# Row tiles in plain order with indexed gathers and chunk-layout copies, instead of rotated and mirrored access patterns

## The chip, the cores and the metric

One core of a Trainium2 chip runs the whole program. The metric is the device time of one execution in microseconds (us). Before the change its median over 3 runs is 2033.77 us (2030.04 to 2036.78).

## The reference

A transformer block with a spectral mixer is computed forward, and then its gradients by all inputs but one:

```
x = A_x
mod = (silu(c) @ w_mod).reshape(c.shape[0], 6, 1, -1)        # sa, ca, ga, sb, cb, gb
h = layernorm(x) * (1 + ca) + sa
x = x + ga * irfft2(rfft2(h) * (w_r + 1j * w_i))             # spectral filter, 2048 x 1024
h = layernorm(x) * (1 + cb) + sb
x = x + gb * (gelu(layernorm(h) @ w1 + b1) @ w2 + b2)        # 1024 -> 3584 -> 1024
out, vjp = jax.vjp(block, A_x, A_w_r, A_w_i, w1, b1, w2, b2, c, w_mod)
return out, *vjp(grad_out)
```

`A_x` and `grad_out` have 2048 rows of 1024 bfloat16 values; `w_r` and `w_i` have 2048 rows of 513.

## The kernel before

The work is written with a tile framework: the code names tiles and operations, and the framework gives every engine its own in-order queue, sets all waits, and lays out each queue by priority and by the time at which it expects an operation to be ready. An engine's order therefore need not be that of the code, but once laid out it is fixed: what waits holds everything behind it on its queue. SyncE's queue (SP) issues loads and DMA transposes, GpSimd's (POOL) issues most stores.

The two-dimensional Fourier transforms are matrix multiplications with cosine and sine matrices that the kernel generates at its start (`trig`, `gen_mats`) and keeps in DRAM (`d_SF`, `d_E`). To make them small, rows are folded: a row tile holds rows n, 2047-n, 1023-n and 1024+n together. Tile i (of 4) has four quarters q of 128 rows each: q = 0 and 3 in natural order (rows 128 i and 1024 + 128 i on), q = 1 and 2 in mirrored order (from row 2047 - 128 i and 1023 - 128 i downwards). `fold_tok`, `fold_d`, `unfold_tok` and `unfold_d` (VectorE) add and subtract quarters and halves of rows.

The stages, in the order of the code:

1. Modulation rows (`mod_block`, L190: 1 MiB blocks `wblkA` and `wblkB` of `w_mod`), loads of `grad_out` (`go`, four tiles) and of `A_x` (`x4`, four tiles in two buffers, `load_x`, L484), generation of the matrices, `d_gBo` = gradient times `gb` (L507) and its DMA transposes `gBoT` (L511), layer norm and folding of x (L522 to L533).
2. Spectral forward (`spectral_core`, L349): `s_fwd`; eight `pair` steps (L354), each of which loads 128 rows of `w_r` and `w_i` twice (`w_plus`, L138, and mirrored `w_minus_parts`, L142) into `ws`, multiplies, and stores `d_P`; `s_inv`; then per row tile the last product into `po`, evacuated by ScalarE (L466), and `consume_fwd` (L543), which loads x again (L547) and stores `d_A`, `d_x1`, `d_n3`.
3. The product of the gradient with the second weight (L573, `wt` by DMA transposes of `B_w2`, result to `d_ph`). It only needs `gBoT` and fills TensorE beside stage 2.
4. The MLP forward and the gradient through the gelu (`z_block`, L599; `bo_pass`, L635, eight of them: `w2` loads L643, half row tiles of `grad_out` L651, `out_0` stored from GpSimd L659).
5. The gradient through the first weight and the layer norms (L706 to L750), per block of 4 x 128 rows: loads of `n3u`, `n2u` and the gradient tile `go4` (L731); stores `d_gx1`.
6. Spectral backward: the same `spectral_core`. Its `pair` steps also load `d_P` into `pf` (L406) and store the gradients of `w_r` and `w_i` (`out_2`, `out_3`) from GpSimd (L414, L416). `consume_bwd` (L771) loads x (L780) and `d_gx1` (L791) and stores `out_1` (L793).
7. Weight gradients: `gw2` (L817, fills TensorE beside stage 6), the gradient of the modulation (L849 to L861), `gw1` (L887).

Everything that reads or writes a row tile goes through `tok_aps` (L116). It puts the rows of a tile on partitions rotated by 64, so that a mirrored quarter is written as two blocks of 64 rows with a row step of -1:

```
out.append((bass.AP(tensor=th, offset=off + r0 * D, ap=[[D, 64], [1024 * D, 2], [1, w]]),
            t4[64 * half:64 * half + 64, 0:4:3, :]))
...
out.append((bass.AP(tensor=th, offset=off + r0 * D, ap=[[64 * D, 2], [-D, 64], [1, w]]), t4[:, q, :]))
```

So a row tile is four DMAs: two of 64 partitions for the natural quarters, and one of 128 rows for each mirrored quarter, whose pattern begins with a dimension of 2. `w_plus` has the same form (128 rows, beginning with a dimension of 2), `w_minus_parts` is two or three DMAs of up to 64 rows. The Fourier matrices are generated for this rotated order (`kev`, `kod`, `rown`, L260 to L272).

Of the kernel before, what the change touches and what calls it, by code (L numbers as in the profile page):

```python
# [16 lines left out]
P = 128  # L17
# [17 lines left out]
def kernel(  # L35
# [62 lines left out]
    d_A = dram.tile([S, D], BF16, name="d_A")  # L98
    d_n3 = dram.tile([S, D], BF16, name="d_n3")
    d_gBo = dram.tile([S, D], BF16, name="d_gBo")  # L100
    d_gx1 = dram.tile([S, D], BF16, name="d_gx1")
# [13 lines left out]

    def tok_aps(dram_, t4, i, c0, c1):  # L116
        s3 = dram_[0] if len(dram_.shape) == 3 else dram_
        th, off = s3.tensor, s3.offset + c0
        lo, w = 128 * i, c1 - c0
        out = []  # L120
        for half in range(2):
            r0 = lo + 64 * (1 - half)
            out.append((bass.AP(tensor=th, offset=off + r0 * D, ap=[[D, 64], [1024 * D, 2], [1, w]]),
                        t4[64 * half:64 * half + 64, 0:4:3, :]))
        for q, top in ((1, 2047), (2, 1023)):
            r0 = top - lo - 64
            out.append((bass.AP(tensor=th, offset=off + r0 * D, ap=[[64 * D, 2], [-D, 64], [1, w]]), t4[:, q, :]))
        return out

    def load_tok(eng, t4, src, i, c0=0, c1=D):  # L130
        for dr, sb in tok_aps(src, t4, i, c0, c1):
            eng.dma_start(out=sb, in_=dr)

    def store_tok(eng, dst, t4, i, c0=0, c1=D):
        for dr, sb in tok_aps(dst, t4, i, c0, c1):
            eng.dma_start(out=dr, in_=sb)  # L136

    def w_plus(w, par, m):  # L138
        r0 = 256 * m + 128 - par
        return bass.AP(tensor=w.tensor, offset=w.offset + r0 * DF, ap=[[128 * DF, 2], [-2 * DF, 64], [1, DF]])  # L140

    def w_minus_parts(w, par, m):  # L142
        out = []
        for half in range(2):
            r0 = 2048 - 256 * m - 128 * (1 + half) + par
            lo = 0
            if half == 1 and par == 0 and m == 3:
                lo = 1
                out.append((64, 65, w[0:1, :]))
            out.append((64 * half + lo, 64 * half + 64,  # L150
                        bass.AP(tensor=w.tensor, offset=w.offset + (r0 + 2 * lo) * DF, ap=[[2 * DF, 64 - lo], [1, DF]])))
        return out

# [105 lines left out]

    kevi = iota([[128, 4], [64, 2], [-1, 64]], 64, 0, 512)  # L260
    kev = to_f(kevi, 512)
    kevc = to_f(kevi, 512)
    nc.gpsimd.memset(kevc[:, 448:449], 0.0)
    kod = gview(512, FP32)
    pts(kod, kev, 2.0, -1.0, ALU.mult, ALU.add)
    pidx = iota([[0, 1]], 64, 1, 1)
    pi2 = gview(1, I32)
    nc.vector.tensor_scalar(out=pi2, in0=pidx, scalar1=127, scalar2=None, op0=ALU.bitwise_and)
    pif = to_f(pi2, 1)
    rown = gview(4, FP32)  # L270
    for i in range(4):
        pts(rown[:, i:i + 1], pif, 2.0, float(256 * i + 1), ALU.mult, ALU.add)  # L272
    rowd = to_f(iota([[256, 2]], 1, 2, 2), 2)
# [75 lines left out]
    def spectral_core(fwd, fb, sms, em, css, pt, evac_u, evac_c, evac_v, consume, o4tag, pfs=None):  # L349
# [4 lines left out]
        def pair(n, par, m):  # L354
            ws = ws2[:, n % 2]
            for x, w in ((0, A_w_r), (1, A_w_i)):
                nc.sync.dma_start(out=ws[:, x, 0, 0:DF], in_=w_plus(w, par, m))
                for lo, hi, src in w_minus_parts(w, par, m):
                    nc.sync.dma_start(out=ws[lo:hi, x, 1, 0:DF], in_=src)
            cs = css[n % 2]  # L360
# [16 lines left out]
            tt(Pt[:, 0:4:3, :], cv[:, 0], cv[:, 1], ALU.subtract)  # L377
            sp_m = par == 0 and m == 3
            if sp_m:
                nc.vector.tensor_copy(out=Pt[64:65, 2:4, :], in_=cv[64:65, 0])  # L380
                nc.vector.tensor_scalar(out=Pt[64:65, 0, :], in0=cv[64:65, 1, 0], scalar1=-1.0, scalar2=None, op0=ALU.mult)
                nc.vector.tensor_copy(out=Pt[64:65, 1, :], in_=cv[64:65, 1, 1])
            Pv = Pt.rearrange("p (s r) w -> p s r w", r=2)[:, :, :, 0:DF]
# [17 lines left out]
            if sp_m:  # L401
                nc.vector.tensor_copy(out=R[64:65, rc, :, 0:DF], in_=qa[64:65, 1, :, 0:DF])
                nc.vector.tensor_copy(out=R[64:65, rs, :, 0:DF], in_=qa[64:65, 0, :, 0:DF])
            if not fwd:
                pf = pfs[n % 2]
                nc.sync.dma_start(out=pf.rearrange("p s r w -> p (s r w)"), in_=d_P[n])  # L406
                m1 = qb2[:, 0]
                m2 = qb2[:, 1]
                tt(m1[:, :, :, 0:DF], Pv, pf[:, :, :, 0:DF], ALU.mult)
                tt(m2[:, :, :, 0:DF], Pv, pf[:, :, ::-1, 0:DF], ALU.mult)  # L410
                tt(pf[:, 0, :, 0:DF], m1[:, :, 0, 0:DF], m1[:, :, 1, 0:DF], ALU.add)
                tt(pf[:, 1, :, 0:DF], m2[:, :, 0, 0:DF], m2[:, :, 1, 0:DF], ALU.subtract)
                for x, w in ((0, out_2), (1, out_3)):
                    nc.gpsimd.dma_start(out=w_plus(w, par, m), in_=pf[:, x, 0, 0:DF])  # L414
                    for lo, hi, dst in w_minus_parts(w, par, m):
                        nc.gpsimd.dma_start(out=dst, in_=pf[lo:hi, x, 1, 0:DF])  # L416

# [62 lines left out]


    x4s = {}
# [152 lines left out]
    def bo_pass(b, h):  # L635
# [22 lines left out]
        tt(bo, bo, x1t, ALU.add)  # L658
        store_tok(nc.gpsimd, out_0, bo, b, h * KH, (h + 1) * KH)  # L659

# [45 lines left out]
    for b in range(NB):  # L706
# [23 lines left out]
        go4 = got[:, 0:4, :]  # L730
        load_tok(nc.sync, go4, grad_out, b)  # L731
        for i in range(4):
# [38 lines left out]
    def consume_bwd(i, o4, tmp, n1):  # L771
# [7 lines left out]
        unfold_tok(o4, tmp)  # L779
        load_tok(nc.sync, n1, A_x, i)  # L780
        norm_act(n1, n1, 0, i)
# [10 lines left out]
        tt(o4, o4, n1, ALU.add)  # L792
        store_tok(nc.gpsimd, out_1, o4, i)  # L793
        if i == 3:
# [130 lines left out]
```

## Time and profile before

| | |
|---|---|
| median of 3 runs | 2033.77 us (2030.04 to 2036.78) |
| the profiled execution, its time | 2022.19 us |
| its span, first to last instruction | 2020.1 us |
| mean granted TensorE clock | 0.88 |
| busy: TensorE / VectorE / ScalarE / GpSimd | 1532.0 / 989.2 / 824.7 / 277.5 us |
| DMA queue of SyncE (hardware) | 362930 packets, 230.27 MB, 46.5% of 16 engines |
| DMA queue of GpSimd (software) | 43040 packets, 108.20 MB, 15.7% |
| row tile loads of x and gradient (L132) | 112 issues |

The views used below: the page (busy time of each engine; the span in 40 slices, each digit the busy share in tenths), windows (busy time of each engine in a stretch), the timeline (start, duration, engine, line, operation, and in brackets how long the engine had been idle and what ended that), the waits (engine and line, what it waited for: total, times, longest), and the groups of instructions (busy time, mean ns). SPq is SyncE's queue: its rows are issues of DMAs, whose duration is that of the issue and not of the transfer. The profile has no landing time for SyncE's DMAs; they are seen in who waits for them.

### The profile page before, as it was taken

How to read it: one execution, taken by the hardware profiler on the slowest of the kernel's cores; microseconds unless marked ns; L12 is line 12 of the kernel's file. 1: busy time of each engine (PE TensorE's matmuls, PEld its weight loads, DVE VectorE, ACT ScalarE, POOL GpSimd, SP SyncE). 2: the span in 40 equal slices, each digit the busy share in tenths (PEclk: the TensorE clock that was granted, in tenths of full speed). 3: DMA queues.
4: the chain of work that ended last, by engine and by line, in shares of the span. 5: the costliest groups of instructions: out<-in, count | busy, mean ns of one | idle time of the engine just before them, and what ended most of it. 6: DMA issues, size and time to landing. Idle time of an engine off the chain costs nothing. (4 is left out here: it accounts for less than half of the span.)

```text
span 2020.1 us, 18395 instructions
## 1 busy us (share of the span) xinstructions
PE 1532.0 (76%) x6722; PEld 686.1 (34%) x6722; DVE 989.2 (49%) x1381; ACT 824.7 (41%) x1095; POOL 277.5 (14%) x423
## 2 busy tenths in 40 slices
PE   2113898767998999999679898376568879925998
PEld 0001354333443344444234343133223334412443
DVE  1143274555138876666403678638555542265100
ACT  2335454676466655555203333243333322263000
POOL 3210010111211111111100000003200111032111
PEclk7556899888999999999889999687788989967999
DMA  6396468568546675656996432545534788598541
GB/s 175 124 214 157 89 159 220 141 209 195 144 120 198 205 227 186 216 188 197 219 247 150 156 122 92 162 102 127 178 97 99 148 226 203 165 331 254 124 122 37
DMA packets 406060, 339.64 MB, mean 168 GB/s; under 512 B 257477, under 2 KB 343493, under 8 KB 405842
## 3 DMA queue, kind: packets, MB, share of 16 engines
q1 hardware_dynamic: 362930, 230.27, 46.5%
q0 software_dynamic: 43040, 108.20, 15.7%
q8 instruction: 52, 0.85, 0.2%
q14 instruction: 38, 0.31, 0.0%
HBM read 168.34 MB, written 112.26 MB: 139 GB/s over the span
## 5 line engine op out<-in xcount | busy, mean ns | idle before, releaser
L887 PE MATMUL gw1acc<-gzs,n3n 128*128 128x512 bf16 x896 | 199.3, 386 | 59.9 <-ACT gwo L891 43.8
L573 PE MATMUL pp<-gBoT,wt 128*128 128x512 bf16 x896 | 209.9, 392 | 31.4 <-ACT phr L575 15.9
L720 PE MATMUL pg<-w1T,gzr 128*128 128x512 bf16 x896 | 201.9, 386 | 4.9 <-DMA gzr<-d_gz 4.8
L887 PEld LDWEIGHTS <-n3n 128*128 128x128 bf16 x896 | 89.0, 99 | 169.8 <-issue 67.3
L158 DVE TENSOR_TENSOR ct<-ct 128x2048 bf16<-128x2048 bf16 (+1 forms) x76 | 103.4, 1388 | 85.5 <-ACT ct L466 62.6
L573 PEld LDWEIGHTS <-wt 128*128 128x128 bf16 x896 | 90.9, 102 | 142.6 <-issue 29.9
L612 PEld LDWEIGHTS <-w 128*128 128x128 bf16 x896 | 87.5, 98 | 122.1 <-issue 20.4
L720 PEld LDWEIGHTS <-gzr 128*128 128x128 bf16 x896 | 89.1, 100 | 115.7 <-issue 8.6
L575 ACT CAST phr<-pp 128x512 bf16<-128x512 f32 x112 | 63.0, 588 | 131.6 <-PE pp L573 71.5
L158 DVE TENSOR_TENSOR gt<-gt,gt 128x2048 bf16<-128x2048 bf16 x84 | 101.9, 1222 | 19.0 <-ACT gt L619 18.1
L647 PEld LDWEIGHTS <-hhA 128*128 128x128 bf16 x704 | 69.5, 99 | 119.4 <-issue 39.1
L612 PE MATMUL pz<-n3Tb,w 128*128 128x512 bf16 x448 | 101.8, 383 | 6.0 <-ACT gt L614 6.0
L817 PE MATMUL gw2acc<-gB,hhsA 128*128 128x512 bf16 x448 | 102.9, 390 | 3.7 <-DMA hhsA<-d_hh 3.7
L817 PE MATMUL gw2acc<-gB,otl 128*128 128x512 bf16 x448 | 102.0, 386 | 3.4 <-ACT gwo L819 3.4
L612 PE MATMUL pz<-n3Ta,w 128*128 128x512 bf16 x448 | 99.9, 379 | 5.5 <-ACT gt L614 5.5
L614 ACT ACTIVATE gt<-pz,b_col 128x512 bf16<-128x512 f32 x112 | 74.5, 682 | 51.3 <-PE pz L612 51.3
L464 PE MATMUL po<-gm,V 128*128 128x256 bf16 x256 | 48.0, 339 | 61.9 <-ACT ct L466 61.6
L429 PE MATMUL pv<-smi,R 128*128 128x512 bf16 x256 | 63.6, 399 | 37.3 <-DVE R L158 36.6
L893 DVE CAST gwo<-gw1acc 128x512 bf16<-128x512 f32 x28 | 19.3, 690 | 148.1 <-PE gw1acc L887 148.1
L576 POOL DMA_DIRECT2D d_ph<-phr x56 | 40.0, 715 | 317.2 <-ACT phr L575 300.8
L891 ACT CAST gwo<-gw1acc 128x512 bf16<-128x512 f32 x28 | 16.3, 584 | 157.8 <-PE gw1acc L887 140.5
L819 ACT CAST gwo<-gw2acc 128x512 bf16<-128x512 f32 x56 | 32.5, 581 | 110.8 <-PE gw2acc L817 109.1
(228 smaller groups left out, 2429.3 us busy)
## 6 DMA issues: line engine op xcount, KB each, us to landing
d_ph<-phr POOLq DMA_DIRECT2D x56, 256.0 KB, 4.6
d_gz<-gt POOLq DMA_DIRECT2D x28, 512.0 KB, 5.1
gzr<-d_gz SPq DMA_DIRECT2D x28, 512.0 KB
wrw<-in_w_mod_dram SPq DMA_DIRECT2D x48, 256.0 KB
out_dram<-gww POOLq DMA_DIRECT2D x48, 256.0 KB, 4.7
d_hh<-hhA POOLq DMA_DIRECT2D x22, 512.0 KB, 4.8
w2sA<-in_B_w_dram SPq DMA_DIRECT2D x19, 512.0 KB
w2sB<-in_B_w_dram SPq DMA_DIRECT2D x19, 512.0 KB
```

What stands on the lines that cost most here:

```text
L158: nc.vector.tensor_tensor(out=out, in0=a, in1=b, op=op)
L429: nc.tensor.matmul(pv[:], lhsT=R[:, cl * 4 + m, :, :].rearrange("p x w -> p (x w)")[:, base:base + 255:2], rhs=smi[:, cl // 2, m, :], star ...
L464: nc.tensor.matmul(po[:, d2 * 256:(d2 + 1) * 256], lhsT=Vs[cl][:, 2 * dc + h, i * P:(i + 1) * P], rhs=gm[:, gi, :], start=(h == 0), stop=( ...
L573: nc.tensor.matmul(pp[:], lhsT=w2t[:, cch, k * P:(k + 1) * P], rhs=gBoT[b][:, cch, :], start=(cch == 0), stop=(cch == NDC - 1))
L575: nc.scalar.copy(out=ph2[:, k, :], in_=pp[:])
L576: nc.gpsimd.dma_start(out=d_ph_v[:, 2 * fg:2 * fg + 2, b * BW:(b + 1) * BW], in_=ph2)
L612: nc.tensor.matmul(pz[:], lhsT=w1s[cch][:, fc * P:(fc + 1) * P], rhs=n3T[:, cch, :], start=(cch == 0), stop=(cch == NDC - 1))
L614: nc.scalar.activation(out=zb[:, k, :], in_=pz[:], func=ACT.Identity, bias=b1_col[:, fc:fc + 1], scale=1.0)
L647: nc.tensor.matmul(pbs[i][:], lhsT=hh[:, k, i * P:(i + 1) * P], rhs=wp[:, k, :], start=False, stop=(g == 6 and k == 3))
L720: nc.tensor.matmul(pgs[i][:], lhsT=gzt[g][:, k, i * P:(i + 1) * P], rhs=w1Ts[g][:, k, h * KH:(h + 1) * KH], start=(g == 0 and k == 0), sto ...
L817: nc.tensor.matmul(acc[:], lhsT=hhs[:, t, k * P:(k + 1) * P], rhs=gBs[t // 4][:, t % 4, h * KH:(h + 1) * KH], start=(t == 0), stop=(t == N ...
L887: nc.tensor.matmul(acc[:], lhsT=n3ns[t // 4][:, t % 4, cch * P:(cch + 1) * P], rhs=gzs[:, t, :], start=(t == 0), stop=(t == NT - 1))
```

## The change

Rows stand on partitions in plain order, and the mirrored quarters are read and written by lists of row numbers. `load_tok`, `store_tok` and `store_tok_half` use one SyncE DMA for the two natural quarters (128 partitions) and two indirect DMAs from GpSimd for the mirrored ones; `w_plus` is one plain DMA on 128 partitions, and the mirrored rows of the weights are gathered and scattered by a list as well. The lists (`xidx`, `oidx`, `widx`) are made once by GpSimd. The Fourier matrices are generated for the plain order, which takes a few operations less.

After its first load each tile of x and of the gradient is stored in DRAM in the layout of its quarters (`d_xp`, `d_go`, by GpSimd), and every later load reads that copy with one plain DMA.

Stores change queues: the natural half of `out_0` and `out_1` and the plain rows of `out_2` and `out_3` are now stored from SyncE; the mirrored rows stay on GpSimd, as scatters. Mirrored loads move from SyncE to GpSimd.

```
-    def tok_aps(dram_, t4, i, c0, c1):
...
+    def load_tok(t4, src, i):
+        s3 = tok_flat(src)
+        nc.sync.dma_start(out=t4[:, 0:4:3, :],
+                          in_=bass.AP(tensor=s3.tensor, offset=s3.offset + 128 * i * D, ap=[[D, P], [1024 * D, 2], [1, D]]))
+        for q in range(2):
+            nc.gpsimd.indirect_dma_start(out=t4[:, 1 + q, :], out_offset=None, in_=s3,
+                                         in_offset=bass.IndirectOffsetOnAxis(ap=xidx[:, 2 * i + q:2 * i + q + 1], axis=0))
+
+    def store_tok(dst, t4, i):
+        s3 = tok_flat(dst)
+        nc.sync.dma_start(out=bass.AP(tensor=s3.tensor, offset=s3.offset + 128 * i * D, ap=[[D, P], [1024 * D, 2], [1, D]]),
+                          in_=t4[:, 0:4:3, :])
+        for q in range(2):
+            nc.gpsimd.indirect_dma_start(out=s3, out_offset=bass.IndirectOffsetOnAxis(ap=xidx[:, 2 * i + q:2 * i + q + 1], axis=0),
+                                         in_=t4[:, 1 + q, :], in_offset=None)
+
+    def store_tok_half(dst, t4, i, h):
...
     def w_plus(w, par, m):
-        r0 = 256 * m + 128 - par
-        return bass.AP(tensor=w.tensor, offset=w.offset + r0 * DF, ap=[[128 * DF, 2], [-2 * DF, 64], [1, DF]])
-
-    def w_minus_parts(w, par, m):
...
+        return bass.AP(tensor=w.tensor, offset=w.offset + (256 * m + par) * DF, ap=[[2 * DF, P], [1, DF]])
+
+    def w_idx(par, m):
+        return bass.IndirectOffsetOnAxis(ap=widx[:, 4 * par + m:4 * par + m + 1], axis=0)
...
-                for lo, hi, src in w_minus_parts(w, par, m):
-                    nc.sync.dma_start(out=ws[lo:hi, x, 1, 0:DF], in_=src)
+                nc.gpsimd.indirect_dma_start(out=ws[:, x, 1, 0:DF], out_offset=None, in_=w, in_offset=w_idx(par, m))
...
-                    nc.gpsimd.dma_start(out=w_plus(w, par, m), in_=pf[:, x, 0, 0:DF])
-                    for lo, hi, dst in w_minus_parts(w, par, m):
-                        nc.gpsimd.dma_start(out=dst, in_=pf[lo:hi, x, 1, 0:DF])
+                    nc.sync.dma_start(out=w_plus(w, par, m), in_=pf[:, x, 0, 0:DF])
+                    nc.gpsimd.indirect_dma_start(out=w, out_offset=w_idx(par, m), in_=pf[:, x, 1, 0:DF], in_offset=None)
...
     def load_x(i):
         x4s[i] = reg.tile([P, 4, D], BF16, name=f"x4_{i}", tag=f"uv{i % 2}")
-        load_tok(nc.sync, x4s[i], A_x, i)
+        load_tok(x4s[i], A_x, i)
+        nc.gpsimd.dma_start(out=chunk_rows(d_xp, i), in_=x4s[i][:])
...
-        load_tok(nc.sync, g4, grad_out, b)
+        load_tok(g4, grad_out, b)
+        nc.gpsimd.dma_start(out=chunk_rows(d_go, b), in_=g4[:])
...
-        load_tok(nc.sync, x4, A_x, i)
+        nc.sync.dma_start(out=x4, in_=chunk_rows(d_xp, i))
...
-        load_tok(nc.sync, go, grad_out, b, h * KH, (h + 1) * KH)
+        nc.sync.dma_start(out=go, in_=chunk_rows(d_go, b)[:, :, cs_])
...
-        store_tok(nc.gpsimd, out_0, bo, b, h * KH, (h + 1) * KH)
+        store_tok_half(out_0, bo, b, h)
...
-        load_tok(nc.sync, go4, grad_out, b)
+        nc.sync.dma_start(out=go4, in_=chunk_rows(d_go, b))
...
-        load_tok(nc.sync, n1, A_x, i)
+        nc.sync.dma_start(out=n1, in_=chunk_rows(d_xp, i))
...
-        store_tok(nc.gpsimd, out_1, o4, i)
+        store_tok(out_1, o4, i)
```

More of the change, by code (lines that the diff above doesn't have):

```diff
@@ L99 @@
     d_n3 = dram.tile([S, D], BF16, name="d_n3")
+    d_xp = dram.tile([S, D], BF16, name="d_xp")
+    d_go = dram.tile([S, D], BF16, name="d_go")
     d_gBo = dram.tile([S, D], BF16, name="d_gBo")
@@ L114, in chunk_rows @@
         return dt[4 * i * P:4 * (i + 1) * P, :].rearrange("(q p) d -> p q d", p=P)
-    def tok_aps(dram_, t4, i, c0, c1):
[L117 to L136, printed above, removed]
-    def w_plus(w, par, m):
-        r0 = 256 * m + 128 - par
-        return bass.AP(tensor=w.tensor, offset=w.offset + r0 * DF, ap=[[128 * DF, 2], [-2 * DF, 64], [1, DF]])
-    def w_minus_parts(w, par, m):
[L143 to L152, printed above, removed]
+    def tok_flat(ap):
+        return ap[0] if len(ap.shape) == 3 else ap
@@ new lines, in store_tok_half @@
+    def store_tok_half(dst, t4, i, h):
+        s3 = tok_flat(dst)
+        nc.sync.dma_start(out=bass.AP(tensor=s3.tensor, offset=s3.offset + 128 * i * D + h * KH, ap=[[D, P], [1024 * D, 2], [1, KH]]),
+                          in_=t4[:, 0:4:3, :])
+        s2 = s3.rearrange("n (h d) -> (n h) d", h=2)
+        for q in range(2):
+            k = 4 * i + 2 * q + h
+            nc.gpsimd.indirect_dma_start(out=s2, out_offset=bass.IndirectOffsetOnAxis(ap=oidx[:, k:k + 1], axis=0),
+                                         in_=t4[:, 1 + q, :], in_offset=None)
@@ L258, in pts @@
         nc.gpsimd.tensor_scalar(out=out, in0=in0, scalar1=s1, scalar2=s2, op0=o0, **kw)
[L260 to L263, printed above, removed]
+    kevc = to_f(iota([[1, 512]], 0, 0, 512), 512)
+    kev = gview(512, FP32)
+    nc.gpsimd.tensor_copy(out=kev, in_=kevc)
+    nc.gpsimd.memset(kev[:, 0:1], 512.0)
     kod = gview(512, FP32)
[L265 to L272, printed above, removed]
+    pts(kod, kevc, 2.0, 1.0, ALU.mult, ALU.add)
+    rown = to_f(iota([[256, 4]], 1, 2, 4), 4)
     rowd = to_f(iota([[256, 2]], 1, 2, 2), 2)
@@ L377, in pair @@
             tt(Pt[:, 0:4:3, :], cv[:, 0], cv[:, 1], ALU.subtract)
[L378 removed]
+            sp_m = par == 0 and m == 0
             if sp_m:
[L380 to L382 removed]
+                nc.vector.tensor_copy(out=Pt[0:1, 0:2, :], in_=cv[0:1, 0])
+                nc.vector.tensor_scalar(out=Pt[0:1, 2, :], in0=cv[0:1, 1, 0], scalar1=-1.0, scalar2=None, op0=ALU.mult)
+                nc.vector.tensor_copy(out=Pt[0:1, 3, :], in_=cv[0:1, 1, 1])
             Pv = Pt.rearrange("p (s r) w -> p s r w", r=2)[:, :, :, 0:DF]
@@ L479, in dve_copy @@
         nc.vector.tensor_copy(out=out, in_=in_)
+    xi = small.tile([P, 32], I32, tag="xi", bufs=1)
+    nc.gpsimd.iota(xi[:, 0:8].rearrange("p (i q) -> p i q", q=2), pattern=[[-128, 4], [-1024, 2]], base=2047, channel_multiplier=-1)
+    nc.gpsimd.iota(xi[:, 8:24].rearrange("p (i q h) -> p i q h", q=2, h=2), pattern=[[-256, 4], [-2048, 2], [1, 2]], base=4094,
+                   channel_multiplier=-2)
+    nc.gpsimd.iota(xi[:, 24:32].rearrange("p (r m) -> p r m", m=4), pattern=[[-1, 2], [-256, 4]], base=2048, channel_multiplier=-2)
+    nc.gpsimd.memset(xi[0:1, 24:25], 1024)
+    xu = const.tile([P, 32], mybir.dt.uint32, name="xu")
+    nc.gpsimd.tensor_copy(out=xu[:], in_=xi[:])
+    xidx, oidx, widx = xu[:, 0:8], xu[:, 8:24], xu[:, 24:32]
     x4s = {}
```

4 lines of the change are left out of this document (2 added, 2 removed).

## The prediction

> **What bounds the kernel now.** I read the page first (busy time, then the 40 slices), then the table by windows of 50 us, then SyncE's queue in order of time, then the waits of single stretches.
>
> ```profile
> span 2020.1 us, 18395 instructions
> PE 1532.0 (76%) x6722; PEld 686.1 (34%) x6722; DVE 989.2 (49%) x1381; ACT 824.7 (41%) x1095; POOL 277.5 (14%) x423
> ...
> PE   2113898767998999999679898376568879925998
> ```
> ```profile
> 0.00:50.00 50.00, 12.83 (x32) 4.53 (x33) 8.24 (x26) 12.69 (x17) 18.87 (x38) 0.71 0.67 177
> 50.00:100.00 50.00, 9.94 (x26) 3.40 (x25) 8.99 (x13) 20.03 (x25) 11.80 (x17) 0.54 0.37 119
> 100.00:150.00 50.00, 8.60 (x26) 2.88 (x25) 24.78 (x26) 17.33 (x26) 10.15 (x6) 0.60 1.03 219
> 150.00:200.00 50.00, 16.47 (x52) 5.67 (x52) 18.97 (x23) 26.88 (x44) 0.00 (x0) 0.67 0.69 160
> ...
> 250.00:300.00 50.00, 50.00 (x233) 27.87 (x232) 34.20 (x48) 27.92 (x50) 6.21 (x10) 1.00 0.56 141
> ...
> 1350.00:1400.00 50.00, 32.92 (x123) 17.67 (x122) 36.38 (x48) 16.65 (x29) 11.36 (x18) 0.80 0.46 112
> 1400.00:1450.00 50.00, 27.19 (x111) 12.02 (x109) 41.68 (x54) 15.31 (x27) 17.78 (x29) 0.74 0.54 141
> ...
> 1800.00:1850.00 50.00, 8.83 (x28) 3.45 (x28) 37.55 (x66) 29.96 (x29) 16.16 (x30) 0.56 0.92 321
> ```
> A window's row gives the busy time of PE, PEld, DVE, ACT and POOL, then the granted clock, the DMA share and GB/s. TensorE is the busy engine, so the time is its 1532 us plus 488 us in which it idles. Of the first 200 us it works 47.84 (12.83 + 9.94 + 8.60 + 16.47), so 152 of the 488 lie there. No engine is full in them, and the DMA engines are full only between 100 and 150 us. What is late is the loading of row tiles:
>
> ```profile
> 2.67 5.45 SPq L132 DMA_DIRECT2D go<-in_grad_out_dram  x4
> ...
> 63.01 28.91 SPq L132 DMA_DIRECT2D go<-in_grad_out_dram  x8
> 92.04 13.19 SPq L192 DMA_DIRECT2D wblkA<-in_w_mod_dram  x2
> 105.33 33.89 SPq L511 DMA_TRANSPOSE gBoT<-d_gBo  x4
> ...
> 201.45 6.79 SPq L567 DMA_TRANSPOSE wt<-in_B_w_dram  x2
> ```
> ```profile
> 28.76 1.06 ACT L311 ACTIVATE n<-x 128x1024 bf16<-128x1024 bf16 x1 [6.12 <-DMA x<-in_A_x_dram]
> ...
> 33.64 1.06 ACT L311 ACTIVATE n<-x 128x1024 bf16<-128x1024 bf16 x1 [2.70 <-DMA x<-in_A_x_dram]
> ...
> 43.23 1.06 ACT L311 ACTIVATE n<-x 128x1024 bf16<-128x1024 bf16 x1 [8.44 <-DMA x<-in_A_x_dram]
> ...
> 109.74 2.29 DVE L158 TENSOR_TENSOR go<-go,rows 128x4096 bf16<-128x4096 bf16 x1 [12.98 <-DMA go<-in_grad_out_dram]
> ```
> The first x tile's natural quarter is there at 28.76, its two mirrored quarters (256 KB each) at 33.64 and 43.23. Six tiles have 12 such quarters, and the last gradient tile is there at 109.74: about 9 us for each quarter, one after the other. Between 50 and 100 us SyncE does nothing but issue, yet the DMA engines are busy 0.37 of the time: a mirrored quarter is not spread over all of them. Everything behind it on SyncE stands in line: the transposes from 105.33, the weights of TensorE's first long work (wt) at 201.45.
>
> **The change part by part.** *Front, tile loads.* A tile's four loads on SyncE become one plain load there, for the natural half, and two gathers on GpSimd's queue; in return each tile is stored once more in chunk layout (8 MiB in all). What must move until the fourth gradient tile is multiplied: 6 MiB of wblkA, 6 tiles, 6 MiB of copies (the multiplication is in place, so it waits until the copy has been read), 18.9 MB. At the 219 GB/s of 100 to 150 us that is 86 us, at the 321 GB/s of 1800 to 1850 us 59 us. I take the middle, 73, as nothing says which holds: 37 us earlier than 109.74. What follows on SyncE (33.89 us of transposes, then the rest up to wt) and on ScalarE and VectorE (the layer norm and folding of four x tiles) keeps its length and moves with it.
>
> ```profile
> ACT n L311 <- DMA x<-in_A_x_dram: 19.0, 5, 5.5
> ```
> This is the wait for the third and fourth x tile, 112 to 217 us. Their natural halves stay behind the transposes, so I take half of it, 9 us, as gain. Two more copies (2.1 MB) cost 10 us of DMA at 219 GB/s; half lies under the layer norm, 5 us lost. Front: 37 + 9 - 5 = 41 us; bounds 110 - 86 + 5 - 10 = 19 and 110 - 59 + 19 - 5 = 65.
>
> *GpSimd's price.* The trace has no gather. Nearest rows:
>
> ```profile
> L414 POOL DMA_DIRECT2D out_dram<-empf x8: 842/847/860, 1368.1 to 1440.7; - x8
> ...
> DMA to landing us min/median/max: 5.6/7.4/11.1
> ```
> ```profile
> L303 POOL TENSOR_SCALAR em<-em 128x2048 bf16<-128x2048 bf16 x1 | 5.4, 5381 | 0.1
> ```
> L414 issues 128 rows of about 1 KB, as a gather does; the other end is the longest GpSimd operation. I take 0.85 us, being the same kind of work; 12 gathers are then 10 us of a queue that is otherwise 14% busy, under the loads' 73 us. At 5.4 us they are 65 us. The generator of matrices loses one wait and a few small operations; nothing waits for it.
>
> *Backward row tiles.* Four iterations load x again, now in one DMA from the copy.
>
> ```profile
> 1496.73 0.37 SPq L791 DMA_DIRECT2D ct<-d_gx  x1
> 1502.44 2.29 DVE L158 TENSOR_TENSOR ct<-ct 128x4096 bf16<-128x4096 bf16 x1 [4.42 <-DMA ct<-d_gx]
> 1505.08 3.29 SPq L132 DMA_DIRECT2D ct<-in_A_x_dram  x4
> 1512.46 1.24 ACT L336 ACTIVATE ct<-ct,stats 128x1024 bf16<-128x1024 bf16 x1 [5.91 <-DMA ct<-in_A_x_dram]
> ...
> 1528.99 1.24 ACT L336 ACTIVATE ct<-ct,stats 128x1024 bf16<-128x1024 bf16 x1 [3.00 <-DMA ct<-in_A_x_dram]
> ```
> ```profile
> PE po L464 <- ACT ct L466: 32.2, 11, 7.3
> ...
> ACT ct L336 <- DMA ct<-in_A_x_dram: 30.2, 7, 9.1
> ...
> ACT ct L466 <- DMA out_dram<-ct: 18.8, 4, 5.7
> ```
> A whole megabyte in chunk layout is used 5.7 us after its issue (d_gx), the same megabyte by mirrored rows 23.9 us after (1505.08 to 1528.99). ScalarE takes its work in order, so these waits hold the evacuation of po, and TensorE waits 32.2 us for that. In that iteration the last part would come some 16 us sooner; I take 10, since the evacuation also waits for the out_1 store (18.8 us in all), and 3 for the other three, which that store limits: 13 us, bounds 5 and 25. The store itself becomes one SyncE store and two scatters; what is behind the SyncE store is the next x load, which needs the same tile anyway.
>
> *Backward layer norm, last block.*
>
> ```profile
> 1261.82 3.53 SPq L727 DMA_DIRECT2D n3u<-d_n  x1
> ...
> 1269.18 0.60 ACT L724 ACTIVATE gn3b<-pg 128x512 bf16<-128x512 f32 x1 [12.00 <-PE pg L720]
> ...
> 1278.46 1.22 DVE L681 CUSTOM_DVE_ANT_0 got<-gn3b,n3u 128x1024 bf16<-128x1024 bf16 x1 [16.02 <-DMA n3u<-d_n]
> ```
> n3u takes 16.6 us from issue to use, behind a gradient tile with mirrored rows. Without it the limit is gn3b, ready at 1269.8: at most 8.7 us, I take 7.
>
> *Forward MLP.*
>
> ```profile
> PE pbo L647 <- DMA w2sA<-in_B_w_dram: 17.7, 3, 13.2
> ...
> PE pbo L647 <- DMA w2sC<-in_B_w_dram: 10.6, 5, 4.1
> PE pbo L647 <- DMA w2sB<-in_B_w_dram: 5.2, 5, 2.9
> ```
> 33.5 us in which TensorE waits for w2 that shares the DMA engines with eight half tiles of the gradient. How much of it is theirs the trace does not say; bounds 0 and 33, I take 4. Against it: the natural half of out_0 now waits on SyncE for VectorE, and ph and w2 loads stand behind it; two scatters wait on GpSimd, and d_hh and d_gz stores stand behind them. I take 3 us lost; if no slot is prefetched, half of L414's 7.4 us of landing in each of eight passes, 30 us.
>
> *Pairs.* Forward, TensorE has the filler L573 beside them, so an earlier or later ws changes nothing. Backward:
>
> ```profile
> DVE qb L158 <- DMA empf<-d_P: 7.5, 3, 6.0
> DVE qb L158 <- DMA pf<-d_P: 5.5, 2, 4.4
> ```
> 13 us could go, as pf waits for old stores; on the other side each pair's SyncE stores now stand ahead of later ws loads. I take nothing, bounds 13 gained and one landing of 7.4 us lost in three pairs, 22.
>
> VectorE was busy 78 of the 100 us from 1350 to 1450, and no L414 issue there took over 860 ns. [...]
>
> Sum: 41 + 13 + 7 + 4 - 3 = 62 us. The profiled execution took 2022.19 (span 2020.1 and 2.1 around it), 11.6 below the median 2033.77. So 1960 as it ran, 1972 as the median.
>
> **The rivals.** *Scatters in a chain, slower.* If every scatter into an output must wait until the write before it to the same tensor has landed, the gathers of the next pair stand behind scatters on GpSimd. Each backward pair then pays two landings, 14.8 us; eight pairs 118, less the 62: 56 slower, 2090. It decides from five pairs of the eight on (74 against 62). For it: the scatters name the whole output. Against it: SyncE's and GpSimd's order is laid out by readiness, so that gathers can go first.
>
> *The copies fill the front.* If everything goes at 219 GB/s, the fourth tile gains 24, the waits 9, and the two later copies take their whole 10; if the transposes' 33.89 us, too, get a third longer beside the copies, 11 more go: 12 for the front. Total 62 - 41 + 12 = 33, time 2001. For it: 100 to 150 us has a share of 1.03. Against it: 321 GB/s at 0.92 later on.
>
> *A dear gather.* At 5.4 us each, the sixth tile is complete after 65 us of issue and one landing, 72, about as forecast; but the two gathers and two scatters of a backward pair hold GpSimd 4 x (5.4 - 0.85) = 18 us longer, half of it on the path: 73 for eight pairs, 11 slower, 2045.
>
> [...]
>
> *More than forecast.* The upper bounds of front, row tiles, layer norm and pairs, and the MLP's 4: 65 + 25 + 9 + 13 + 4 = 116 us, 1918.
>
> **How the numbers follow.** Forecast 0.56; more than forecast 0.08; copies 0.14; held gathers 0.08; scatter chain 0.10; dear gather 0.04. A measurement here tells about 0.3%, 6 us, from no change. The range leaves out half of the best case and the two slower rivals (0.18): 1925 to 2034, where the unknown costs have eaten everything. Slower: 0.14, and 0.01 of the milder cases, 0.15; same, out of those, 0.04; faster 0.81.
>
> **What would show it.** Right: the fourth gradient tile's multiplication near 73 us, wt's first use 30 to 50 us earlier than 208, TensorE's idle time before it shorter, ScalarE's 30.2 us wait for x under 10, n3u's 16.0 gone. Wrong: gathers of several us; GpSimd waiting for DMA before scatters; VectorE waiting for ws in the backward pairs; 0 to 100 us with a DMA share near 1 and no earlier transposes.

## The result, and the profile after

The changed kernel takes 1919.55 us (median of 4 runs, 1912.43 to 1925.1) against 2035.28 us for the kernel before beside it: a ratio of 0.943, 95% interval 0.939 to 0.947. It is faster by 116 us. The forecast was 1972, with a range from 1925 to 2034; the direction was right, the gain nearly twice what was forecast, and the median lies 5 us below the range. The profiled execution took 1915.37 us, its span 1913.6, which is 106.5 less than before. The profiled execution of before was 13 us under its median and that of after 4 under its own, so the stretches below add up to 106.5 and not to 116.

The page's first lines and the busy tenths of TensorE and of the DMA engines, after:

```profile
span 1913.6 us, 18102 instructions
...
PE 1514.3 (79%) x6590; PEld 681.7 (36%) x6722; DVE 991.2 (52%) x1380; ACT 826.9 (43%) x1097; POOL 353.2 (18%) x422
...
PE   2328998778988999998688999295479998817998
...
DMA  9994485694365576657993444424636678698551
```
TensorE does the same work (6722 weight loads in both; 132 matmul records are missing here); what went is idle time. GpSimd has 76 us more to do and is still 82% idle. The DMA row begins with three nines, where the forecast had found the engines half empty. The windows of the front:

```profile
0.00:50.00 50.00, 15.45 (x46) 5.72 (x47) 8.85 (x26) 19.94 (x29) 27.32 (x46) 0.79 1.03 337
50.00:100.00 50.00, 16.76 (x45) 5.43 (x44) 30.36 (x34) 30.72 (x39) 33.63 (x31) 0.64 1.06 249
100.00:150.00 50.00, 19.00 (x65) 7.44 (x68) 17.41 (x19) 17.80 (x28) 14.02 (x13) 0.62 1.13 279
150.00:200.00 50.00, 43.18 (x196) 19.25 (x198) 19.71 (x20) 36.02 (x62) 5.79 (x8) 1.00 0.33 92
```
337, 249 and 279 GB/s, where it was 177, 119 and 219, and TensorE works 43 of the 50 us from 150 on (16.47 before). The timeline of the fourth gradient tile, of SyncE's transposes and of TensorE's first long work:

```profile
68.48 2.28 DVE L157 TENSOR_TENSOR go<-go,rows 128x4096 bf16<-128x4096 bf16 x1
```
```profile
34.38 27.12 SPq L569 DMA_TRANSPOSE wt<-in_B_w_dram  x2
73.09 4.14 SPq L513 DMA_TRANSPOSE gBoT<-d_gBo  x1
...
82.83 21.18 SPq L513 DMA_TRANSPOSE gBoT<-d_gBo  x1
...
104.72 20.71 SPq L513 DMA_TRANSPOSE gBoT<-d_gBo  x2
```
```profile
144.66 8.80 PE L575 MATMUL pp<-gBoT,wt 128*128 128x512 bf16 x39
```
The gradient tile is there at 68.48 instead of 109.74 (the forecast said near 73). The transposes of wt, which stood at 201.45, have moved ahead of gBoT on SyncE: the framework laid the queue out anew.

To see where the rest lies, I cut both executions at the same instructions: the first product of the spectral core (pcs), the last product of the filler (pp), the first one of the gradient through w1 (pg), the last two of the spectral backward (pu, pv), the first of gw1. The table has the lengths of the stretches in us.

| stretch | before | after | gain | forecast |
|---|---|---|---|---|
| front, to the first pcs | 252.1 | 206.5 | 45.6 | 41 |
| spectral forward with its filler, to the last pp | 323.4 | 295.2 | 28.2 | 0 |
| MLP, to the first pg | 467.1 | 475.5 | -8.4 | 1 |
| backward layer norm, to the last pu | 310.4 | 290.9 | 19.5 | 7 |
| backward pairs, to the last pv | 108.0 | 109.6 | -1.6 | 0 |
| backward row tiles and gw2, to gw1 | 289.3 | 265.2 | 24.1 | 13 |
| gw1 to the end | 269.8 | 270.7 | -0.9 | 0 |
| sum | 2020.1 | 1913.6 | 106.5 | 62 |

Single stretches move by some us between versions in which nothing of theirs was changed (the MLP's has 465 to 476 in the runs below, gw1's 267.7 to 274.0), so I read nothing into less than 8 us of one stretch. The stretches of the experiments are cut in the same way.

### The profile page after: what moved, and what is told of

Its sections match the earlier page's. It is cut to its first block, busy times and chain, and to the rows that moved or that the text cites. A ratio compares the mean times of both kernels' runs of the same rounds, so it can differ in the third digit from the quotient of the medians.

```text
span 1913.6 us, 18102 instructions
## 1 busy us (share of the span) xinstructions
PE 1514.3 (79%) x6590; PEld 681.7 (36%) x6722; DVE 991.2 (52%) x1380; ACT 826.9 (43%) x1097; POOL 353.2 (18%) x422
## 5 line engine op out<-in xcount | busy, mean ns | idle before, releaser
L575 PE MATMUL pp<-gBoT,wt 128*128 128x512 bf16 x875 | 202.5, 387 | 15.9 <-ACT phr L577 14.8
L893 ACT CAST gwo<-gw1acc 128x512 bf16<-128x512 f32 x28 | 16.3, 584 | 157.1 <-PE gw1acc L889 140.7
```

The costliest lines, as they stand in the source:

```text
L575: nc.tensor.matmul(pp[:], lhsT=w2t[:, cch, k * P:(k + 1) * P], rhs=gBoT[b][:, cch, :], start=(cch == 0), stop=(cch == NDC - 1))
```

## The experiments

Three theories stood at the start. *A:* a mirrored transfer issued by SyncE runs on few DMA engines and is slow; it does not matter what takes its place. *B:* the gathers are needed for the gain. *C:* the gain behind the front is that of the copies, one plain transfer in place of four. A fourth, *D*, was for the 23 us by which TensorE's first long product came earlier (208.79 to 144.66) beyond the 41 of the gradient tile: SyncE's new order. Ratios are to the kernel before, run beside each.

**1. The loads by themselves.**

```
for f in (plain, gap2, mir2, mir4, mir8, mir16, mirpool, gath):
    group([f] * 4)                    # four loads of 128 rows x 2 KB, then read
group([mir2, mir2, plain, plain])
group([mir2, mir2, gath, gath])
```

> Loads alone, nothing else computed (the outputs are left out but for one row). Ten groups of four loads of 128 rows of 2 KB (1 MB in all), each group begun only when the group before it has been read: plain rows; two blocks of 64 rows in natural order, with a gap; mirrored as in the kernel before (2 blocks of 64 rows, row step -1), then 4 blocks of 32, 8 of 16, 16 of 8; the mirrored pattern of before from GpSimd's queue; gathers by row number; two mirrored and two plain loads on SyncE; two mirrored loads on SyncE beside two gathers. Theory A (the leading dimension of 2 of the pattern puts a transfer on few DMA engines): mirrored in two blocks some 9 us a load, about 36 a group, and the natural order in two blocks as much; 4 blocks half of it, 18; 8 blocks 9; 16 blocks and plain rows 5 to 7; in the mixed group the plain loads come as late as the mirrored ones. Rival B (the negative row step is what costs): natural order in two blocks 5 to 7 us, and all four mirrored forms about 36. Gathers: 4 issues of about 1 us and one landing, 8 to 12 us by both. From GpSimd's queue the mirrored pattern takes 36 by A and B alike if the pattern alone decides, and 8 to 12 if it is SyncE's queue that spreads by the leading dimension.

VectorE reads the four tiles of a group in order, so the starts of its reads are the arrivals. Lines of the timeline: the last two arrivals of natural order in two blocks, of mirrored in two blocks, of four blocks and of 16 blocks; the issues and the last arrival of the old pattern on GpSimd's queue; the first issue and the last arrival of the gathers; the middle two arrivals of the first mixed group:

```profile
25.37 0.17 DVE L107 COPY acc<-tb 128x2 bf16<-128x2 bf16 x1 [5.09 <-DMA tb<-in_grad_out_dram]
30.63 0.17 DVE L107 COPY acc<-tb 128x2 bf16<-128x2 bf16 x1 [5.08 <-DMA tb<-in_grad_out_dram]
...
49.69 0.17 DVE L107 COPY acc<-tb 128x2 bf16<-128x2 bf16 x1 [5.09 <-DMA tb<-in_grad_out_dram]
54.95 0.17 DVE L107 COPY acc<-tb 128x2 bf16<-128x2 bf16 x1 [5.09 <-DMA tb<-in_grad_out_dram]
...
66.23 0.17 DVE L107 COPY acc<-tb 128x2 bf16<-128x2 bf16 x1 [2.46 <-DMA tb<-in_grad_out_dram]
68.86 0.17 DVE L107 COPY acc<-tb 128x2 bf16<-128x2 bf16 x1 [2.46 <-DMA tb<-in_grad_out_dram]
...
83.70 0.17 DVE L107 COPY acc<-tb 128x2 bf16<-128x2 bf16 x1 [0.79 <-DMA tb<-in_grad_out_dram]
84.45 0.17 DVE L107 COPY acc<-tb 128x2 bf16<-128x2 bf16 x1 [0.58 <-DMA tb<-in_grad_out_dram]
...
85.15 3.41 POOL L76 DMA_DIRECT2D tb<-in_grad_out_dram  x4 [83.92 <-DVE tb L109]
...
97.16 0.17 DVE L107 COPY acc<-tb 128x2 bf16<-128x2 bf16 x1 [0.82 <-DMA tb<-in_grad_out_dram]
...
98.37 1.05 POOL L100 DMA_INDIRECT tb<-in_grad_out_dram,xu  x1 [9.80 <-DVE tb L109]
...
105.80 0.17 DVE L107 COPY acc<-tb 128x2 bf16<-128x2 bf16 x1 [1.02 <-DMA tb<-in_grad_out_dram,xu]
...
119.91 0.17 DVE L107 COPY acc<-tb 128x2 bf16<-128x2 bf16 x1 [4.96 <-DMA tb<-in_grad_out_dram]
120.57 0.17 DVE L107 COPY acc<-tb 128x2 bf16<-128x2 bf16 x1 [0.49 <-DMA tb<-in_grad_out_dram]
```
And the windows inside the mirrored group of two blocks and that of four:

```profile
40.00:54.00 14.00, 0.35 (x2) 0.00 (x0) 1.00 0.13 50
62.00:68.50 6.50, 0.34 (x2) 0.00 (x0) 1.00 0.25 94
```
With nothing else running a mirrored quarter costs 5.26 us (54.95 - 49.69), where theory A had said 9, at 50 GB/s and a DMA share of 0.13, an eighth: as much as two of 16 engines. In natural order, two blocks cost the same 5.26. Four blocks 2.63 at a share of 0.25, 16 blocks under 1 for the last. So the leading dimension decides and not the direction; the rival of the negative step falls. That the 9 us of the front are this with other transfers on the same engines is likely, but no run shows it by itself. On GpSimd's queue four old patterns are there 12.0 us after the first issue (97.16 - 85.15), the four gathers 7.4 us (105.80 - 98.37). In the mixed group the first plain load is read 0.66 us after the second mirrored one; as VectorE reads in order, it may have landed earlier: whether it was held stays open.

**2 and 3. The front's mirrored quarters alone**, by the old pattern on GpSimd's queue, then by gathers; everything else is before. Eight tiles with sixteen mirrored quarters are loaded there (the second expectation says ten tiles).

```
-        load_tok(nc.sync, g4, grad_out, b)       # and x4s[i]
+        load_front(g4, grad_out, b)
...
+    for k, (dr, sb) in enumerate(tok_aps(src, t4, i, 0, D)):      # front_swq
+        (nc.sync if k < 2 else nc.gpsimd).dma_start(out=sb, in_=dr)
...
+    nc.gpsimd.indirect_dma_start(out=t4[:, 1 + q, :], ...)        # front_gather, q = 0, 1
```

> The kernel before with one edit: the twelve mirrored quarters that are loaded in the front, and the later ones of x there, go from SyncE to GpSimd's queue, in the same pattern; later re-reads, weights and stores are as before. If the slow thing is the pattern on SyncE's queue: the last gradient tile is multiplied near 70 us instead of 109.7, the first long work of TensorE begins 35 to 45 us earlier, and the time falls by about 40 us, to 1995. If the pattern is slow on either queue: the gradient tile stays near 100 and the time within 10 us of before. If gathers are needed for the gain: as before, too.

> The kernel before with one edit: the mirrored quarters of the front's ten row tile loads are gathered by row number on GpSimd's queue (lists for the rotated order); everything else, the two loads of 64 partitions for the natural half and all later mirrored loads among it, as before. If all that matters is that the mirrored pattern leaves SyncE's queue: as the run with the same quarters in the old pattern from GpSimd, 1992, first long work near 175.7. If the gather itself is the better transfer: 1965 to 1980, first long work near 155.

By the old pattern 1992.18 us, ratio 0.982 (0.977 to 0.987); by gathers 1964.74, ratio 0.964 (0.961 to 0.967). The queue alone gives 26 us of the front stretch (252.1 to 226.1), the gathers 35 more (191.2). So A is only half of it, and B the other half, in the front: the two-block pattern stays slow on GpSimd's queue once the front is busy. DMA issues and landing times (last column, us), the pattern in the loaded front and alone:

```profile
go<-in_grad_out_dram POOLq DMA_DIRECT2D x8, 256.0 KB, 21.4
```
```profile
tb<-in_grad_out_dram POOLq DMA_DIRECT2D x4, 256.0 KB, 8.8
```
From 50 to 100 us the pattern's version has a DMA share of 1.18 and moves 228 GB/s, the gathers' version 1.12 and 283. The four transposes behind them take 54.06 us and 37.82.

**4. The copies alone.**

```
+        nc.gpsimd.dma_start(out=chunk_rows(d_go, b), in_=g4[:])    # and d_xp
...
-        load_tok(nc.sync, go4, grad_out, b)                       # all later reads
+        nc.sync.dma_start(out=go4, in_=chunk_rows(d_go, b))
```

> The kernel before with the chunk copies of x and of the gradient added, and every later read from them in one transfer; the front's mirrored loads, the weights and the stores stay as before. If the gain behind the front (42 us in the comparison of the two traces: 10 in the forward spectral stage, 20 in the backward layer norm, 24 in the backward row tiles, less 10 in the MLP) comes from re-reads that are no longer mirrored: 2035 less 35 to 45 and up to 10 more for the copies in the front, 1995 to 2010. If it comes from the earlier front, the new store queues or the weights: within 10 us of before.

2007.57 us, ratio 0.988 (0.984 to 0.992). The front gets 21.9 us longer (274.0), and behind it 37 us go: layer norm 292.1, row tiles and gw2 278.6, spectral forward 317.6. That is 37 of the 60.9 us that the whole change gains behind the front, but the next run shows that most of it does not need a copy.

**5. All of the change but the copies.**

```
-        nc.gpsimd.dma_start(out=chunk_rows(d_go, b), in_=g4[:])    # and d_xp
...
-        nc.sync.dma_start(out=n1, in_=chunk_rows(d_xp, i))         # all later reads
+        load_tok(n1, A_x, i)
```

> The kernel after without the chunk copies: every later read of a row tile is again by rows, a plain half on SyncE and two gathers on GpSimd. If what counted was that no mirrored pattern stands on SyncE any more: within 10 us of after, 1910 to 1930. If the one-transfer read of the copies made the 42 us behind the front: 1950 to 1965. If the copies cost time in the front (8.4 MB at 249 to 337 GB/s are 25 to 34 us of the DMA engines): the last gradient tile is multiplied some 15 us earlier than 68.5.

1920.38 us, ratio 0.946 (0.942 to 0.951): the same as after, but by another way. The fourth gradient tile is multiplied at 36.78 instead of 68.48, the first pcs at 187.0 instead of 206.5, and at the last pv it is 29.0 us ahead (1348.7 against 1377.7). Then it loses them all: row tiles and gw2 take 298.3 against 265.2. Behind the front this version, too, is 37 us ahead of before: 38.6 in the spectral forward stage (284.8) and 14.2 in the layer norm (296.2), less 9.0 in the row tiles and some 7 elsewhere. So C falls but for the row tiles. In the layer norm it is enough that the pattern goes: VectorE's wait for n3u, 44.8 us in that stretch before and 44.2 with gathers in the front alone, is gone with the copies and without them. Before:

```profile
DVE got L681 <- DMA n3u<-d_n: 44.8, 3, 16.0
```
The waits of the row tiles, without the copies and after:

```profile
ACT ct L337 <- DMA ct<-in_A_x_dram,xu: 41.5, 6, 10.3
PE po L463 <- ACT ct L465: 40.1, 11, 8.9
...
POOL ct L124 <- DVE ct L165: 19.6, 3, 9.0
```
```profile
ACT ct L457 <- DMA out_dram<-ct: 16.3, 3, 6.7
PE po L455 <- ACT ct L457: 15.1, 8, 4.3
...
ACT ct L329 <- DMA ct<-d_xp: 1.1, 1, 1.1
```
Gathered x makes ScalarE wait 41.5 us, more than mirrored x did (30.2); from the copy 1.1. These gathers stood behind no scatter: on GpSimd's queue they waited for VectorE to free their buffer (19.6 us). For the third tile they were issued at 1448.14 and 1449.46, and ScalarE came to the second quarter only at 1462.83; why it took that long was not tried.

**6 and 7. Only the copy of x**, made in the front, or at x's second read.

```
         load_tok(x4, A_x, i)                                       # consume_fwd
+        nc.gpsimd.dma_start(out=chunk_rows(d_xp, i), in_=x4)       # x_copy_later
```

> The kernel after with the copy of x alone (made in the front), and no copy of the gradient, which is read by rows each time. The version without any copy began TensorE's first long work at 120.0 against 144.7, and lost 33 us again from the last backward pair to the last weight gradient. If the gradient's copy is worth nothing later: first long work at 125 to 135, the backward row tiles as in after, time 1900 to 1912. If the gradient's copy carried the later gain: 1925 to 1940.

> As the version without copies, but x is stored in chunk layout when the forward row tiles read it for the second time, behind TensorE's filler, and the backward row tiles read that copy. If the copies cost only where nothing covers them: first long work at 120, backward row tiles as in after, 1885 to 1900. If storing the copy (about 9 us from issue to landing, before the in-place addition) delays the forward row tiles in the open: up to 4 x 9 = 36 us of it are lost, 1920.

1905.64 us, ratio 0.938 (0.935 to 0.940), and 1898.59, ratio 0.932 (0.931 to 0.934). Both beat both kernels; the second is the best version of the study. First pp at 128.3 and 126.2, row tiles and gw2 at 270.4 and 266.2. The gradient's copy gave back less than it cost in the front. Between the two, x's copy at its second read gains 6.9 us in the front (193.3 against 200.2) and 4.2 in the row tiles, but it is not free: the spectral forward stage takes 299.9 against 283.1, and the filler's wait for its store is 40.9 us there against 7.7. The two profiled spans are 1904.3 and 1901.5, so the 7 us by which the second is ahead stand in the medians alone.

**8 to 10. SyncE's order (D).** wt early in the kernel before, and late in the kernel after, in two ways.

```
+    for fg in range(2):                                            # wt_early, ahead of gBoT
+        nc.sync.dma_start_transpose(out=wt[:, fg], in_=B_w2[fg * 256:(fg + 1) * 256, :])
...
+        nc.vector.tensor_copy(out=wt[0:1, k, 0, 0:2], in_=fbuf[0:1, 3, 0, 0:2])  # wt_late
...
+        nc.vector.tensor_copy(out=wt[0:1, k, 0, 0:2], in_=fbuf[0:1, 1, 0, 0:2])  # wt_behind_ws
```

> The kernel before with one edit: the first two transposes of the second weight (wt) are written, and issued by SyncE, ahead of the transposes of the gradient instead of some 96 us behind them; loads, copies and stores as before. If SyncE's order alone was a brake: the first long work of TensorE follows the gradient's transposes, near 165 us instead of 208.8, and the time falls by 20 to 40 us, to 1995 to 2015. If the x tiles that the spectral stage needs set its pace anyway: the product starts earlier but the spectral stage does not, TensorE only fills idle time sooner, and the time falls by less than 15 us.

> The kernel after, with the first two transposes of the second weight (wt) made to wait for the folding of the fourth x tile, as late as they stood in the kernel before (VectorE writes two elements of each buffer first, which the transposes overwrite). If SyncE's new order (wt ahead of gBoT) is what gave the 23 us by which the front gained more than its last gradient tile did (64.1 against 41.3): the first long work of TensorE begins 15 to 25 us later than 144.7 and the time is 1935 to 1945. If that gain lies elsewhere: within 6 us of after, 1914 to 1926.

> The kernel after, with the first two wt transposes placed on SyncE where they stood before, behind the gm transposes and the first four ws loads, but with no later wait: they now wait (by two elements per buffer that VectorE writes) for the folding of the second x tile, done at 126 us in after. If SyncE's order is worth what the queue says: wt is issued near 150, 27 us of transposes that stood ahead of gBoT are gone there, first long work at 150 to 160 instead of 144.7, time 1920 to 1932. If the order was worth the whole 23 us of the front's extra gain: first long work at 165 to 170, time 1938 to 1945. If gBoT's transposes start earlier without wt ahead of them and carry the rest along: no loss, 1912 to 1922.

wt_early: 2019.13, ratio 0.9945 (0.991 to 0.998). First pp 19 us earlier, first pcs 9, the end 5. wt_late: 1941.64, ratio 0.953 (0.950 to 0.956), as D had said, but it overshot: wt went out at 185.79, and pp began at 215.4, behind the first pcs. wt_behind_ws has wt at 155.03, right behind ws as before: first pp 160.7, 16 us later than in after, the first pcs 5.8 later, and yet 1918.39 in all, ratio 0.946 (0.942 to 0.950), the same as after. So D falls as the source of 23 us. An earlier first product is worth little by itself (0.2 to 0.9% in wt_early); it is filler. It costs more only when it comes so late that filler is missing ahead of the spectral core (wt_late has 129 of its weight loads more behind the first pcs than after, 1295 against 1166, and 26.9 us more there).

**11 to 13. The queue of the plain stores.**

```
-        nc.sync.dma_start(out=bass.AP(tensor=s3.tensor, ...), in_=t4[:, 0:4:3, :])   # out_0, out_1
+        nc.gpsimd.dma_start(out=bass.AP(tensor=s3.tensor, ...), in_=t4[:, 0:4:3, :])
...
-                    nc.sync.dma_start(out=w_plus(w, par, m), ...)                    # out_2, out_3
+                    nc.gpsimd.dma_start(out=w_plus(w, par, m), ...)
```

> The kernel after with the plain stores of out_0, out_1, out_2 and out_3 issued from GpSimd, as before, and the scatters behind them on the same queue. The stretch of the backward row tiles and the rest of gw2 took 289.3 us before, 278.6 with the copies alone and 265.2 after; the copies explain 10.7 of the 24.1. If the other 13 come from the plain stores having left GpSimd's queue (the next tile's evacuation waits for the out_1 store): 275 to 280 in that stretch and 8 to 15 us slower than after, 1928 to 1935. If they come from the scatters and plain rows in place of mirrored stores: that stretch within 4 us of 265, time 1914 to 1924. If the 8 us that the MLP stage lost to the stores on SyncE come back with it: 467 instead of 475.5 there, and up to 8 us faster.

> The kernel after with only the natural half of out_0 issued from GpSimd again. With all plain stores there the MLP stage took 468.1 instead of 475.5, and the backward pairs 124.9 instead of 109.6. If the store of out_0 on SyncE costs the MLP stage its 8 us, and the stores of the pairs alone cause the loss in the pairs: MLP stage 467 to 469, pairs 108 to 111, time 1908 to 1914. If the MLP stage varies by that much with the order alone: 1914 to 1924, MLP stage 472 to 478.

> The version that copies x at its second read, with the plain stores on GpSimd's queue as well: the likeliest best of the versions if stores on SyncE cost the MLP stage time. If they do: 1885 to 1895 against 1898.6. If their queue does not matter: 1893 to 1906. If scatters behind plain stores on one queue hold the backward row tiles: 1906 to 1915.

All stores back on GpSimd, in the kernel after: 1938.57, ratio 0.955 (0.949 to 0.960); in the best version 1918.36, ratio 0.944 (0.938 to 0.951). out_0 alone: 1915.81, ratio 0.943 (0.941 to 0.945), the same as after. The loss is in the backward pairs: 124.9 and 125.2 us against 109.6 and 108.4; row tiles and gw2 take 269.6 and 269.3 against 265.2 and 266.2. The 269.6 lie between the two forecasts, so what the queue of the stores is worth there stays open. The waits of the pairs, after and with the stores on GpSimd:

```profile
DVE qb L157 <- DMA empf<-d_P: 12.8, 3, 9.8
```
```profile
DVE qb L157 <- DMA empf<-d_P: 30.7, 3, 10.4
```
A later pair's d_P lands in the buffer that these stores read, so stores that go out later hold it. This is read from the waits: SyncE's load of d_P waits 25.3 us for the scatters from that buffer in after and 46.3 us with the stores on GpSimd. The MLP's 475.5 is not the price of the out_0 store: wt_behind_ws has that store on SyncE too and takes 465.2.

## Why the forecast was right in kind and short in size

*Front, tile loads* (37 + 9 - 5 = 41): right in the mechanism and the sum. The tile came 41 us earlier, the first pcs 45.6. What the first experiment shows for "a mirrored quarter is not spread over all of them" is a DMA share of 0.13 with two blocks, at 5.26 us a quarter, and of 0.25 with four, at 2.63. The sentence "keeps its length and moves with it" failed: SyncE's order changed, and the transposes of the gradient took from 73.09 to 125.43, 52 us instead of 33.89. Against that, ScalarE's wait for the third and fourth x tile (19.0, of which half was booked) is gone altogether, and the copies cost 19.5 us and not 5 beside the tiles. That the sum came so close is in part luck.

*"Forward, TensorE has the filler L573 beside them, so an earlier or later ws changes nothing"*: this is the step that failed first. It was said of ws, and the whole stage was then booked at nothing; its second read of x, in `consume_fwd`, appears in no term. The stage gained 28.2 us. The filler is not only cover, it is also held up. The waits of this stretch, before, after, and with the copies alone:

```profile
ACT phr L575 <- DMA d_ph<-phr: 59.9, 16, 11.0
...
PE pp L573 <- ACT phr L575: 15.9, 7, 5.4
...
PE pv L429 <- DVE R L158: 7.1, 2, 5.9
```
```profile
ACT phr L577 <- DMA d_ph<-phr: 24.5, 9, 7.7
...
PE pp L575 <- ACT phr L577: 8.5, 5, 2.9
...
PE pv L420 <- DVE R L157: 2.2, 1, 2.2
```
```profile
ACT phr L579 <- DMA d_ph<-phr: 18.6, 6, 4.6
...
PE pv L431 <- DVE R L160: 6.7, 2, 5.8
PE pp L577 <- ACT phr L579: 6.1, 3, 3.1
```
The filler's evacuation waits for its own store (d_ph). The wait is 49 to 60 us in every version that reads x there by the old pattern (before, wt_early, both front versions) and 18.6 with the copies alone, so the mirrored reads of x in `consume_fwd` hold that store up; that they do so on the shared DMA engines is inferred. TensorE feels less of it: its own wait for the evacuation falls from 15.9 to 8.5. The other part of the 28 is work that had already been done: of pp's and the core's weight loads 1225 lay in this stretch before and 1166 after; 59 at 0.22 us (270.5 us of TensorE for 1226 matmuls before) are 13 us. These 13 and 15 us of idle time make the 28. With the copies alone, which leave the weights' loads as they were, TensorE idles 43.9 us of the stretch instead of 52.9: 9 of the 15 are x's. Of the rest, 5 us are its wait for VectorE's R (7.1 before, 6.7 with the copies alone, 2.2 after), while VectorE's own waits for ws fall from 17.6 us to 1.8, so a later ws did change something; that part was read from the waits and not run alone.

*Backward layer norm* (7, "at most 8.7 us"): mis-sized, 19.5. The forecast looked at one of four blocks; n3u's wait was 44.8 us over three blocks in this stretch, and it is gone. The copies alone give 18.3 of it (292.1), gathers without copies 14.2.

*Backward row tiles* (13, bounds 5 and 25): mis-sized, 24.1, inside the bounds. ScalarE's wait for x went from 30.2 to 1.1 as said. The copies alone give 10.7. The other 13 stay open. ScalarE does not wait less for the out_1 store (18.8 us before, 16.3 + 9.1 after), yet TensorE's wait for the evacuation falls from 32.2 us to 26.3 with the copies alone, 24.1 with all stores on GpSimd and 15.1 after. So the forecast's 3 for the three other iterations, "which that store limits", was too small, and no run shows by itself what the new store pattern or its queue is worth there.

*MLP and pairs* (4 - 3 and 0): -8.4 and -1.6. The w2 waits (33.5 us) stayed, 18.4 + 8.1 + 10.0 = 36.5, so the 4 us for the gradient's half tiles were wrong; the rest is within what this stretch varies by. In the backward pairs VectorE waits for no ws at all, so the sign that the prediction set against itself there stayed away.

*The rivals.* Held gathers, whose chance of 0.08 was an estimate that no run bears out, and the dear gather cost nothing that the pairs show (1.6 us longer): but for three (last section) a gather took 0.94 to 2.03 us. The copies do fill the front, and cost 19.5 us there (206.5 against 187.0), but with a better front beneath them. The scatter chain exists: GpSimd waits 32.8 us in the pairs for the plain stores, as these lines of its waits show, and yet the stretch is hardly longer, because TensorE and VectorE mostly wait for other things.

```profile
POOL out_dram L407 <- DMA out_dram<-pf: 20.0, 3, 9.3
...
POOL out_dram L407 <- DMA out_dram<-empf: 12.8, 3, 7.7
```
"More than forecast" came out nearest (its 1918 against 1919.55), but that is luck: its terms were others. Front and forward gave 73.8 instead of 65 for the front, the layer norm 19.5 instead of 9, the MLP and the pairs nothing, and only the row tiles fit (24.1 against 25).

## What to carry to other kernels

Look at the leading dimension of every DMA pattern: with 2 there, 256 KB on SyncE's queue took 5.3 us alone, at a DMA share of 0.13, and some 9 in the front of before; the sign there was a share of 0.37 from 50 to 100 us beside a queue that did nothing but issue. When such a pattern goes, loads and stores of others can gain too (with the copies alone the wait for n3u fell from 44.8 us to none and that for d_ph from 59.9 to 18.6), so price the waits for other transfers in each stage too, and count filler as something that can be held up. A scratch copy pays only where its reader is waited for: leaving out the gradient's copy gave 14 us, making x's copy later 7 more.

## What was not expected of the hardware

A gather took 0.94 to 1.43 us for the row tiles of the front, and 0.95 to 2.03 us for the weights but for three: 7.41 and 8.37 us in the forward pairs and 11.09 us in the backward ones. GpSimd's lines, and VectorE's operations around the longest:

```profile
1286.33 11.09 POOL L351 DMA_INDIRECT ws<-in_A_w_r_dram,xu  x1 [6.61 <-DMA out_dram<-empf]
1297.72 0.99 POOL L407 DMA_INDIRECT out_dram<-empf,xu  x1 [0.30 <-issue]
...
1311.17 1.45 POOL L351 DMA_INDIRECT ws<-in_A_w_i_dram,xu  x1 [0.30 <-issue]
```
```profile
1293.03 1.28 DVE L157 TENSOR_TENSOR pf<-qb 128x1026 bf16<-128x1026 bf16 x2
1294.24 1.22 DVE L157 TENSOR_TENSOR qa<-Pt,ws 128x2052 bf16<-128x2052 bf16 x1
1295.38 1.21 DVE L157 TENSOR_TENSOR qb<-Pt,ws 128x2052 bf16<-128x2052 bf16 x1
1306.36 1.23 DVE L157 TENSOR_TENSOR qb<-Pt,empf 128x2052 bf16<-128x2052 bf16 x1 [9.77 <-DMA empf<-d_P]
```
The gather ends at 1297.42, 0.83 us after VectorE's unbroken row of two-input operations (1296.59); the next indirect DMA, a scatter beside an idle VectorE, takes 0.99. Such a row by itself does not make a gather long: the gather at 1311.17 runs wholly beside one, too (VectorE is busy with two-input operations from 1306.36 on, past the gather's end), and takes 1.45 us. What makes the three so long stays open; that VectorE holds them is not shown. They cost nothing that can be seen: VectorE waits 1.8 us for gathered weights in the whole kernel.
